# Half tiles of 64 tokens in an attention kernel: two heads in one unit of 128 partitions

## The chip, the cores and the metric

The kernel runs on one core of one Trainium2 chip. The metric is the device time of one execution in microseconds, the median of several runs. Five engines work side by side on a core: TensorE (PE, with PEld for its weight loads), VectorE (DVE), ScalarE (ACT), GpSimd (POOL) and SyncE (SP), which issues all DMAs here.

## The reference

Attention with rotary positions over 4 batches, 8 heads, 576 positions and a head width of 64, then a two-layer network with a leaky ramp on the 2304 tokens of 512 values:

```python
q_rot, k_rot = rotate(q), rotate(k)
scores = q_rot @ k_rot.T / sqrt(D)              # (4, 8, 576, 576)
attn = exp(scores - max(scores)); attn = attn / (sum(attn) + 1e-09)
x = (attn @ v).transpose(0, 2, 1, 3).reshape(B * S, H * D)
h = x @ w_in                                    # (2304, 512) @ (512, 2048)
g = maximum(h, 0.0) + alpha * minimum(h, 0.0)
return g @ w_out                                # (2304, 2048) @ (2048, 512)
```

## The kernel before

The 2304 tokens are cut into 18 tiles of 128. A batch has 576 tokens, four tiles and a half, so tiles 4 and 13 lie across two batches and are cut into two parts of 64 tokens, with partitions 0 to 63 for the first batch and 64 to 127 for the second. All other tiles are one part. Two tiles form a block of 256 tokens, nine in all.

Attention works on pairs of heads. `pair` (L642) takes one part of a tile and two heads that share a tile of keys (`ks`, one head on rows 0 to 63, the other on rows 64 to 127). It issues four score products (L653, two halves of 288 keys for each head, on 64 rows of the array, fp32), each head into its own two banks of PSUM. The products always take all 128 tokens of the tile, the other batch's too, and `head` (L661) then uses the partitions `a:z` of the part. For each head `head` makes one unit: maximum over the 576 scores (L665, VectorE), exponential with its sum (L674, ScalarE), the fp16 high part (L679, ScalarE or VectorE), the low part (L693, VectorE), a transpose by DMA (L697, SyncE) and 14 products with the values (L703). With 64 tokens a unit is as long as with 128; it only uses half the partitions. Each of tiles 4 and 13 has 2 parts x 8 heads = 16 such units, a whole tile has 8, so there are 160 units in all. `normalise` (L710) scales a part's sums by 1/sum (`rs`, shown at the line of the helper `scalar`, L352) and splits the result into fp16 high and low (`xs`, L722 and L724), which are transposed into `xt`.

`expert` (L736) does the network for one block in 16 slices of 128 hidden values: twelve products of layer 1 (L745, in two halves of six), the ramp on ScalarE (L756) and VectorE (`r`, L759), and layer 2. For blocks 0 and 1 layer 2 is two fp32 products of 512 columns (L765, two instructions each); from block 2 on it is six products (L783) of `r` split into `gh` and `gl`. Attention of block i + 1 runs between the slices of block i. The first quarter of the span also loads the weights and converts them from 64-bit words, mostly on VectorE (L506 to L515, L580, L584).

Nothing is ordered by hand. `Plan` (L68) collects all operations with a due time, the engines that may do them and a modelled cost, and runs a model of the five engines that picks the next operation for each; the program is issued in that order. The table `PRM` (L35) holds due times and costs. VectorE and GpSimd are modelled as taking turns on one port, except for operations marked `port=False`; `small` (L347) marks its VectorE operations so, among them `rs`. Each buffer is reused in the order of the plan, and an operation waits for the users of the buffer before.

## Time and profile before

| | us |
|---|---|
| median of 3 runs | 695.69 |
| lowest, highest | 694.82, 698.32 |
| the profiled execution, its own time | 700.17 |
| its span, first to last instruction | 698.4 |

| engine | busy, us | share of the span |
|---|---|---|
| TensorE | 620.2 | 89% |
| VectorE | 522.8 | 75% |
| ScalarE | 354.7 | 51% |
| GpSimd | 194.8 | 28% |

Busy time is the time in which an engine executes. A product is given an end by a model, so a busy TensorE may still be short of its peak. "Idle before" is the time in which the engine had nothing to do just before a group, and the releaser is what ended the wait. The granted clock (PEclk) is a share of TensorE's full 2.4 GHz.

### The profile page before, as it was taken

How to read it: one execution, taken by the hardware profiler on the slowest of the kernel's cores; microseconds unless marked ns; L12 is line 12 of the kernel's file. 1: busy time of each engine (PE TensorE's matmuls, PEld its weight loads, DVE VectorE, ACT ScalarE, POOL GpSimd, SP SyncE). 2: the span in 40 equal slices, each digit the busy share in tenths (PEclk: the TensorE clock that was granted, in tenths of full speed). 3: DMA queues.
4: the chain of work that ended last, by engine and by line, in shares of the span. 5: the costliest groups of instructions: out<-in, count | busy, mean ns of one | idle time of the engine just before them, and what ended most of it. 6: DMA issues, size and time to landing. Idle time of an engine off the chain costs nothing.

```text
span 698.4 us, 14088 instructions
## 1 busy us (share of the span) xinstructions
PE 620.2 (89%) x5448; PEld 445.0 (64%) x5448; DVE 522.8 (75%) x898; ACT 354.7 (51%) x799; POOL 194.8 (28%) x149
## 2 busy tenths in 40 slices
PE   0756678769998999999999999999999999999997
PEld 0434444346555666776767777776777777777775
DVE  5988999999889876768896485777976757765332
ACT  3536756549763535444664544444665444643322
POOL 3753100204735331235623121352232212010000
PEclk9965569979999999999999999999999999999999
DMA  8999798685885676547896465683466545453000
GB/s 291 309 228 215 156 290 217 184 263 130 143 185 97 119 129 137 94 99 176 199 206 106 99 112 98 119 180 47 78 108 115 100 77 93 100 110 58 31 1 31
DMA packets 209523, 96.48 MB, mean 138 GB/s; under 512 B 192304, under 2 KB 196528, under 8 KB 209456
## 3 DMA queue, kind: packets, MB, share of 16 engines
q1 hardware_dynamic: 209456, 95.59, 63.0%
q8 instruction: 42, 0.69, 0.4%
q14 instruction: 25, 0.20, 0.1%
HBM read 41.56 MB, written 4.72 MB: 66 GB/s over the span
## 4 chain that ended last, share of the span: by engine, by line
PE 62%; DMA 17%; DVE 16%; issue 2%; SPq 1%; ACT 1%; POOL 0%; ACTq 0%; DVEq 0%; POOLq 0%
PE h L745 22%; PE pair L783 20%; DMA pt<-pp 11%; PE pair L653 8%; PE v L703 7%; PE pair L765 5%; DVE pp L693 3%; DVE mx L665 2%; DMA wraw<-in_moe_w_in_dram 2%; DMA qr<-in_q_dram 1%; DMA kraw<-in_k_dram 1%; DVE wi L584 1%; DVE wo L515 1%; DVE r L759 1%; DVE pp L352 1%
## 5 line engine op out<-in xcount | busy, mean ns | idle before, releaser
L745 PE MATMUL h<-xt,wi 128*128 128x256 f16 x1728 | 231.1, 277 | 14.8 <-DVE r L759 14.4
L745 PEld LDWEIGHTS <-wi 128*128 128x128 f16 x1728 | 155.8, 99 | 76.2 <-issue 59.0
L674 ACT ACTIVATE e<-pair,mx 128x576 f32<-128x576 f32 (+1 forms) x160 | 117.2, 736 | 89.2 <-DVE mx L665 85.7
L693 DVE SCALAR_TENSOR_TENSOR pp<-e,pp 128x576 f16<-128x576 f32 (+1 forms) x160 | 136.0, 858 | 13.6 <-ACT pp L679 11.9
L759 DVE SCALAR_TENSOR_TENSOR r<-r,beta,h 128x256 f32<-128x256 f32 x144 | 68.6, 476 | 78.7 <-ACT r L756 78.0
L665 DVE TENSOR_REDUCE mx<-pair 128x1 f32<-128x576 f32 (+1 forms) x160 | 114.1, 750 | 13.3 <-PE pair L653 12.6
L703 PE MATMUL v<-vv,pt 128*128 128x64 f16 (+1 forms) x2240 | 93.5, 198 | 30.1 <-DMA pt<-pp 29.7
L756 ACT ACTIVATE r<-h 128x256 f32<-128x256 f32 x144 | 55.1, 382 | 127.5 <-PE h L745 125.0
L703 PEld LDWEIGHTS <-pt 128*128 128x128 f16 (+1 forms) x2240 | 83.8, 104 | 56.4 <-DMA pt<-pp 43.7
L653 PE MATMUL pair<-ks,qn 64*128 64x288 f32 x640 | 112.4, 458 | 5.8 <-ACT e L674 4.8
L783 PE MATMUL pair<-wh,gh 128*128 128x512 f32 x224 | 96.4, 430 | 0.1
L783 PE MATMUL pair<-wh,gl 128*128 128x512 f32 x224 | 88.8, 397 | 1.6 <-POOL gl L776 1.6
L776 POOL TENSOR_TENSOR gl<-r,gh 128x256 fp32r<-128x256 f32 x55 | 53.3, 969 | 129.4 <-ACT gh L773 108.4
L783 PE MATMUL pair<-wo,gh 128*128 128x512 f32 x224 | 88.1, 393 | 0.0
L653 PEld LDWEIGHTS pair<-ks,qn 64*128 64x128 f32 x640 | 61.4, 198 | 40.8 <-issue 15.1
L679 ACT ACTIVATE pp<-e 128x576 f16<-128x576 f32 (+1 forms) x97 | 65.5, 681 | 19.6 <-DMA pt<-pp 15.6
L773 ACT ACTIVATE gh<-r 128x256 fp32r<-128x256 f32 x100 | 41.7, 417 | 56.7 <-PE pair L783 28.6
L765 PE MATMUL pair<-wo,r 128*128 128x512 f32 x128 | 63.4, 622 | 0.0
L783 PEld LDWEIGHTS pair<-wh,gl 128*128 128x128 f32 x224 | 42.3, 189 | 12.2 <-POOL gl L776 2.4
L724 POOL TENSOR_TENSOR xs<-y,xs 128x512 f16<-128x512 f32 (+1 forms) x18 | 25.2, 1398 | 86.5 <-DVE xs L722 65.1
L783 PEld LDWEIGHTS pair<-wh,gh 128*128 128x128 f32 x224 | 42.5, 190 | 10.4 <-issue 2.7
L636 POOL TENSOR_TENSOR qn<-qr 128x512 f32<-128x512 f32 (+1 forms) x19 | 24.0, 1265 | 87.7 <-PE pair L653 87.7
(70 smaller groups left out, 533.8 us busy)
## 6 DMA issues: line engine op xcount, KB each, us to landing
kraw<-in_k_dram SPq DMA_DIRECT2D x16, 576.0 KB, 4.8
qr<-in_q_dram SPq DMA_DIRECT2D x18, 512.0 KB, 4.3
wraw<-in_moe_w_in_dram SPq DMA_DIRECT2D x16, 512.0 KB, 5.7
wraw<-in_moe_w_out_dram SPq DMA_DIRECT2D x16, 512.0 KB, 6.5
vraw<-in_v_dram SPq DMA_DIRECT2D x16, 320.0 KB, 4.3
out_dram<-os SPq DMA_DIRECT2D x18, 256.0 KB, 2.6
pt<-pp SPq DMA_TRANSPOSE x160, 3.4
vv<-vv SPq DMA_DIRECT2D x32, 64.0 KB, 2.2
```

Of the source, the lines that this page charges most:

```text
L653: nc.tensor.matmul(out=ps[h]()[:, x, :HS], lhsT=qn()[r, p], rhs=kt()[r, x * HS:(x + 1) * HS], start=True, stop=True)
L665: lambda e: nc.vector.tensor_reduce(out=mx()[a:z], in_=ps()[a:z, :, :HS], axis=AX.XY, op=ALU.max, negate=True),
L674: lambda e: nc.scalar.activation(out=ex()[a:z].rearrange("p (x c) -> p x c", x=2), in_=ps()[a:z, :, :HS], func=ACTF.Exp, bias=mx()[a:z], a ...
L679: lambda e: nc.scalar.activation(out=pp()[a:z, 0], in_=ex()[a:z], func=ACTF.Copy, scale=1.0 if early else E_SC) if e == ACT
L693: lambda e: nc.vector.scalar_tensor_tensor(out=pp()[a:z, 1], in0=ex()[a:z], scalar=E_SC, in1=pp()[a:z, 0], op0=ALU.mult, op1=ALU.subtract),
L703: nc.tensor.matmul(out=v_b()[a:z, i], lhsT=pt()[:, s, :z - a], rhs=vt()[:, h, w], start=(n == 0), stop=(n == len(order) - 1))
L745: nc.tensor.matmul(out=ps(), lhsT=wi_b()[:, kk, j // FG, w, f], rhs=x()[:, y * KC + kk], start=(kk == 0 and n == 0), stop=(kk == KC - 1 an ...
L756: lambda e: nc.scalar.activation(out=g(), in_=ps(), func=ACTF.Relu, scale=-1.0),
L759: lambda e: nc.vector.scalar_tensor_tensor(out=g(), in0=g(), scalar=beta_b()[:, j:j + 1], in1=ps(), op0=ALU.mult, op1=ALU.add),
L765: nc.tensor.matmul(out=po()[:, x], lhsT=g()[:, x * 128:(x + 1) * 128], rhs=wf[j](), start=(j == 0), stop=(j == KF - 1))
L776: lambda e: ENG[e].tensor_tensor(out=gl(), in0=g(), in1=gh().bitcast(F32), op=ALU.subtract),
L783: nc.tensor.matmul(out=po()[:, x], lhsT=s()[:, ts], rhs=w, start=(j == 0 and c == 0), stop=(j == KF - 1 and c == 2))
```

## The change

A part of 64 tokens goes to the new `half_pair`. It keeps a square of 128 x 128 for each pair of heads (`qd`, one buffer for a part's four pairs): the 64 queries of the first head stand in rows and columns 0 to 63, those of the second in rows and columns 64 to 127, and the rest is zero. ScalarE copies the queries in (two copies a part), GpSimd or VectorE fills in the zeros (two fills a part). Two score products on all 128 rows then give both heads, the first on partitions 0 to 63, the second on 64 to 127, in one PSUM bank pair. `head` is called once for both heads, so a part has 4 units instead of 8; 144 are left in all. The sums of a part go into a tile `st` with a column for each pair, and two VectorE copies a part bring them to the partitions where `normalise` reads them (`sums`). The weighted sums are still two runs of 14 products, one for each head, from the two halves of the unit's transposed tile.

The table's new numbers are `wl2` 12.07, `wb2` 4.87, `kd` 2.73, `wg` 3.2, `ph0` 3.06, `lw` 3.8, `la` 2, `ka` 2.03, `vp` 1.47 and `gl` 10.88.

```diff
--- before.py
+++ after.py
-PRM = {"qd": 7.03, "qd0": 3.48, "vl0": 32.45, "wl": 12.02, "wl2": 24.13, "wb": 10.45, "wb2": 4.75, "ws": -0.7, "ws2": -0.08, "kl": 40.87, "vl": 40.84, "lead": 3.61, "flow": 4, "pen": -3.74, "ph": 1.2, "xlo": 1.8, "kd": 3.03, "pl": 1.01, "wlo": 16.77, "wg": 2.88, "bk": 1500, "lead1": 2.25, "ph0": 4.16, "nb": 1, "wh": 8.51, "lw": 3.65, "pvd": 4.03, "pw": 3.28, "la": 4, "lv": 1, "nks": 5, "nvv": 5, "ka": 6.08, "va": 0.1, "vc": -2.76, "vp": 1.57, "qa": 0.5, "qr": 78.54, "tqk": 1340, "l2d": 3.34, "tl2": 1400, "nos": 2, "nr": 2, "fo": 4, "fi": 4, "gh": 21.96, "gl": 11.78, "gh0": -1.64, "gl0": 1.86, "tp": 0, "nf": 2, "sh": 8.29, "sl": 2.28, "tl": 0, "wpe": 0, "vpe": 1, "wk": 4.09}
+PRM = {"qd": 7.03, "qd0": 3.48, "vl0": 32.45, "wl": 12.02, "wl2": 12.07, "wb": 10.45, "wb2": 4.87, "ws": -0.7, "ws2": -0.08, "kl": 40.87, "vl": 40.84, "lead": 3.61, "flow": 4, "pen": -3.74, "ph": 1.2, "xlo": 1.8, "kd": 2.73, "pl": 1.01, "wlo": 16.77, "wg": 3.2, "bk": 1500, "lead1": 2.25, "ph0": 3.06, "nb": 1, "wh": 8.51, "lw": 3.8, "pvd": 4.03, "pw": 3.28, "la": 2, "lv": 1, "nks": 5, "nvv": 5, "ka": 2.03, "va": 0.1, "vc": -2.76, "vp": 1.47, "qa": 0.5, "qr": 78.54, "tqk": 1340, "l2d": 3.34, "tl2": 1400, "nos": 2, "nr": 2, "fo": 4, "fi": 4, "gh": 21.96, "gl": 10.88, "gh0": -1.64, "gl0": 1.86, "tp": 0, "nf": 2, "sh": 8.29, "sl": 2.28, "tl": 0, "wpe": 0, "vpe": 1, "wk": 4.09}
...
+    qd_T = tag("qd", 1, [128, NP, 128], F32)
+    st_T = tag("st", 2, [128, NP], F32)
...
     def pair(at, step, t, b, p, a, z, banks):
-        if t not in sums:
-            sums[t], ys[t], xss[t], vos[t] = sums_T.new(), y_T.new(), xs_T.new(), v_T.new()
         kt, vt, qn = ks[b, p], vv[b, p], qs[t]
+        if z - a < 128:
+            return half_pair(at, t, b, p, a, z, banks[p % 2])
         ps = [x.new() for x in banks]
...
-    def head(at, t, p, h, a, z, ps, vt):
-        sm, v_b, i = sums[t], vos[t], 2 * p + h
+    qds, sts = {}, {}
+
+    def half_pair(at, t, b, p, a, z, bank):
+        kt, vt, qn = ks[b, p], vv[b, p], qs[t]
+        if (t, a) not in qds:
+            qd, sts[t, a] = qd_T.new(), st_T.new()
+            qds[t, a] = qd
+            for h in range(2):
+                o, c = 64 * h, 64 - 64 * h
+                op(at - 2, {POOL: 420, DVE: (t_dve(256, fast=True), 1)},
+                   lambda e, o=o, c=c: ENG[e].memset(qd()[o:o + 64, :, c:c + 64], 0.0), writes=[(qd, h)])
+                op(at - 2, {ACT: t_act(256)},
+                   lambda e, o=o: nc.scalar.activation(out=qd()[o:o + 64, :, o:o + 64], in_=qn()[o:o + 64, :, a:z], func=ACTF.Copy),
+                   reads=[(qn, 0), (qn, 2)], writes=[(qd, 2 + h)])
+        qd, ps = qds[t, a], bank.new()
+
+        def scores(e):
+            for x in range(2):
+                nc.tensor.matmul(out=ps()[:, x, :HS], lhsT=qd()[:, p], rhs=kt()[:, x * HS:(x + 1) * HS], start=True, stop=True)
+
+        op(at, {PE: 980}, scores, kind=WIDE, reads=[(qd, x) for x in range(4)] + [kt], writes=[ps])
+        head(at, t, p, None, a, z, ps, vt)
+        if p == NP - 1:
+            st, sm = sts[t, a], sums[t]
+            for h in range(2):
+                small(at + 0.8, lambda h=h: nc.vector.tensor_copy(
+                    out=sm()[a:z].rearrange("p (c x) -> p c x", x=2)[:, :, h], in_=st()[64 * h:64 * h + 64]),
+                    reads=[(st, x) for x in range(NP)], writes=[(sm, (2 * x + h, a)) for x in range(NP)])
+            normalise(at + 0.8, t, b, a, z)
+
+    def head(at, t, p, h, c, d, ps, vt):
+        both = h is None
+        a, z = (0, 128) if both else (c, d)
+        if t not in sums:
+            sums[t], ys[t], xss[t], vos[t] = sums_T.new(), y_T.new(), xs_T.new(), v_T.new()
+        v_b = vos[t]
+        if both:
+            acc, acc_of = lambda: sts[t, c]()[:, p:p + 1], (sts[t, c], p)
+        else:
+            acc, acc_of = lambda: sums[t]()[a:z, 2 * p + h:2 * p + h + 1], (sums[t], (2 * p + h, a))
...
-               bias=mx()[a:z], accum_out=sm()[a:z, i:i + 1]),
-           reads=[ps, mx], writes=[ex, (sm, (i, a))])
+               bias=mx()[a:z], accum_out=acc()),
+           reads=[ps, mx], writes=[ex, acc_of])
...
-        def pv(e):
-            order = [(s, s) for s in [0, *range(NH, NSEG), *range(1, NH)]] + [(s, NSEG + s) for s in range(NH)]
+        order = [(s, s) for s in [0, *range(NH, NSEG), *range(1, NH)]] + [(s, NSEG + s) for s in range(NH)]
+
+        def pv(e, g, o):
             for n, (s, w) in enumerate(order):
                 nc.tensor.matmul(
-                    out=v_b()[a:z, i], lhsT=pt()[:, s, :z - a], rhs=vt()[:, h, w],
+                    out=v_b()[c:d, 2 * p + g], lhsT=pt()[:, s, o:o + d - c], rhs=vt()[:, g, w],
                     start=(n == 0), stop=(n == len(order) - 1))
 
-        op(at + (0.6 if t < 4 else PRM["pvd"]), {PE: 430}, pv, kind=SHORT,
-           reads=[pt] + [(vt, x) for x in range(4)], writes=[(v_b, (i, a))])
+        for g, o in [(0, 0), (1, 64)] if both else [(h, 0)]:
+            op(at + (0.6 if t < 4 else PRM["pvd"]), {PE: 430}, lambda e, g=g, o=o: pv(e, g, o), kind=SHORT,
+               reads=[pt] + [(vt, x) for x in range(4)], writes=[(v_b, (2 * p + g, c))])
```

The order that the plan makes of it, at three places. First VectorE in the middle of block 0's experts, where the last slices of `w_in` and `w_out` are converted (`wraw`, `wi`, `wo`); `r` is the ramp's result, which layer 2 and the next layer 1 wait for. Before:

```order
L515 SCALAR_TENSOR_TENSOR wraw<-wraw,wi 128x512
L511 SCALAR_TENSOR_TENSOR wo<-wraw,wo 128x512
L693 SCALAR_TENSOR_TENSOR pp<-e,pp 128x576
L515 SCALAR_TENSOR_TENSOR wo<-wraw,wo 128x512
L540 TENSOR_REDUCE cm<-wm 128x1
L506 TENSOR_SCALAR wo<-wraw 128x512
L364 STREAM_TRANSPOSE ct<-cm 128x32
L759 SCALAR_TENSOR_TENSOR r<-r,beta,h 128x256
```

After:

```order
L735 SCALAR_TENSOR_TENSOR pp<-e,pp 128x576
L517 SCALAR_TENSOR_TENSOR wraw<-wraw,wi 128x512
L508 TENSOR_SCALAR wo<-wraw 128x512
L803 SCALAR_TENSOR_TENSOR r<-r,beta,h 128x256
L513 SCALAR_TENSOR_TENSOR wo<-wraw,wo 128x512
L542 TENSOR_REDUCE cm<-wm 128x1
L508 TENSOR_SCALAR wo<-wraw 128x512
```

The `r` has moved ahead of two steps of the conversion of `wo` and of the first steps that find the weights' bound.

Second VectorE where the first part of tile 4 ends. `sums` are the sums of exponentials, `rs` their reciprocal, `ve` the bound of the next batch's values. Before:

```order
L364 STREAM_TRANSPOSE ct<-cm 128x32
L365 TENSOR_REDUCE cr<-ct 128x1
L357 MEMSET cm 128x32
L693 SCALAR_TENSOR_TENSOR pp<-e,pp 64x576
L759 SCALAR_TENSOR_TENSOR r<-r,beta,h 128x256
L352 TENSOR_SCALAR ve<-pair_2038 128x1
L352 TENSOR_SCALAR rs<-sums 64x8
L352 TENSOR_SCALAR ve<-ve 128x1
L715 RECIPROCAL rs<-rs 64x8
```

After:

```order
L393 TENSOR_TENSOR ks<-kraw 128x576
L366 STREAM_TRANSPOSE ct<-cm 128x32
L393 TENSOR_TENSOR ks<-kraw 128x576
L690 COPY sums<-st 64x4 x2
L367 TENSOR_REDUCE cr<-ct 128x1
L735 SCALAR_TENSOR_TENSOR pp<-e,pp 128x576
L354 TENSOR_SCALAR rs<-sums 64x8
```

The two copies of the sums stand ahead of `rs`, between two additions of the rotated keys (`ks`) and the search for the values' bound.

Third the beginning of tile 13. `kraw` are the keys times the rotation table, `xs` the high part of the tile before, `gl` the low part of `r`. VectorE before:

```order
L717 TENSOR_TENSOR y<-v,rs 128x512
L722 CAST xs<-y 128x512
L759 SCALAR_TENSOR_TENSOR r<-r,beta,h 128x256
L724 TENSOR_TENSOR xs<-y,xs 128x512
L665 TENSOR_REDUCE mx<-pair_5923 64x1
L391 TENSOR_TENSOR ks<-kraw 128x576
L665 TENSOR_REDUCE mx<-pair_5925 64x1
```

VectorE after:

```order
L707 TENSOR_REDUCE mx<-pair_5777 128x1
L390 TENSOR_TENSOR kraw<-kraw,tab 128x1152
L354 TENSOR_SCALAR pp<-e 128x576
L761 TENSOR_TENSOR y<-v,rs 128x512
L803 SCALAR_TENSOR_TENSOR r<-r,beta,h 128x256
L735 SCALAR_TENSOR_TENSOR pp<-e,pp 128x576 x2
L803 SCALAR_TENSOR_TENSOR r<-r,beta,h 128x256
```

GpSimd at the same place, before:

```order
L391 TENSOR_TENSOR ks<-kraw 128x576
L776 TENSOR_TENSOR gl<-r,gh 128x256
L388 TENSOR_TENSOR kraw<-kraw,tab 128x1152
L776 TENSOR_TENSOR gl<-r,gh 128x256
L391 TENSOR_TENSOR ks<-kraw 128x576
```

and after:

```order
L393 TENSOR_TENSOR ks<-kraw 128x576
L820 TENSOR_TENSOR gl<-r,gh 128x256 x2
L393 TENSOR_TENSOR ks<-kraw 128x576
L768 TENSOR_TENSOR xs<-y,xs 128x512
L820 TENSOR_TENSOR gl<-r,gh 128x256
L675 MEMSET qd 64x4x64 x2
L820 TENSOR_TENSOR gl<-r,gh 128x256 x2
```

The multiplication `kraw` has moved from GpSimd to VectorE, ahead of `y`; VectorE's CAST of `xs` is gone from it (ScalarE does it now), and GpSimd does the low part of `xs` and the zero fills.

## Rows read from the trace of the kernel before

**Rows 1.** The page, part 1: engine, busy us, share of span, instructions.

```profile
PE 620.2 (89%) x5448; PEld 445.0 (64%) x5448; DVE 522.8 (75%) x898; ACT 354.7 (51%) x799; POOL 194.8 (28%) x149
```

**Rows 2.** Stretches: length; busy us (instructions) by engine; PEclk, DMA share, GB/s.

```profile
149.90:264.20 114.30, 106.25 (x930) 66.38 (x928) 99.25 (x164) 66.56 (x143) 46.77 (x28) 0.99 0.71 137
...
264.20:466.60 202.40, 196.24 (x1863) 149.55 (x1861) 146.43 (x253) 103.53 (x245) 65.37 (x55) 1.00 0.66 134
...
466.60:575.70 109.10, 106.41 (x1020) 79.86 (x1019) 82.61 (x141) 56.08 (x132) 29.83 (x26) 0.98 0.52 91
...
475.00:480.00 5.00, 5.00 (x30) 3.59 (x27) 3.69 (x7) 2.81 (x7) 0.00 (x0) 0.72 0.56 55
```

**Rows 3.** The chain that ended last: start us, us, engine, tile, line, instructions.

```profile
213.33 1.72 PE pair L765 x4
...
215.05 1.17 PE pair L653 x8
...
456.67 1.42 PE h L745 x12
...
482.82 1.40 PE pair L783 x6
...
490.20 1.00 PE v L703 x28
...
516.08 0.56 PE v L703 x14
```

**Rows 4.** Groups by line and shape: count, busy us, mean ns, idle before, releaser.

```profile
L665 DVE TENSOR_REDUCE mx<-pair 64x1 f32<-64x576 f32 x32 | 23.0, 749 | 3.9 <-PE pair L653 3.6
...
L693 DVE SCALAR_TENSOR_TENSOR pp<-e,pp 64x576 f16<-64x576 f32 x32 | 27.1, 858 | 4.8 <-ACT pp L679 4.4
...
L756 ACT ACTIVATE r<-h 128x256 f32<-128x256 f32 x144 | 55.1, 382 | 127.5 <-PE h L745 125.0 <-PE pair L765 1.5 <-POOL gl L776 0.2
...
L388 DVE TENSOR_TENSOR kraw<-kraw,tab 128x1152 f32<-128x1152 f32 x4 | 5.8, 1442 | 2.5 <-DMA kraw<-in_k_dram 2.5
...
L722 DVE CAST xs<-y 128x512 f16<-128x512 f32 x11 | 6.9, 630 | 0.1
...
L357 POOL MEMSET cm<- 128x32 f32 x6 | 0.9, 156 | 59.0 <-DVE ct L364 58.7 <-POOLq L924 0.3
...
L773 ACT ACTIVATE gh<-r 128x256 fp32r<-128x256 f32 x100 | 41.7, 417 | 56.7 <-PE pair L783 28.6 <-DVE r L759 26.8
...
L352 DVE TENSOR_SCALAR rs<-sums 128x8 f32<-128x8 f32 x16 | 4.2, 264 | 0.9 <-ACT e L674 0.9
```

**Rows 5.** Timeline of TensorE, 149.9 to 264.2 us: start us, us, work, [idle before, releaser].

```profile
152.20 0.82 PE L745 MATMUL h<-xt,wi 128*128 128x256 f16 x6 [2.26 <-DVE r L759]
...
164.02 0.81 PE L745 MATMUL h<-xt,wi 128*128 128x256 f16 x6 [0.91 <-DVE r L759]
...
207.09 0.63 PE L703 MATMUL v<-vv,pt 128*64 128x64 f16 x14 [1.23 <-DMA pt<-pp]
...
225.36 1.47 PE L745 MATMUL h<-xt,wi 128*128 128x256 f16 x12 [1.75 <-DVE r L759]
```

**Rows 6.** Timeline of VectorE and GpSimd in the same stretch.

```profile
151.71 0.43 DVE L759 SCALAR_TENSOR_TENSOR r<-r,beta,h 128x256 f32<-128x256 f32 x1
...
222.42 2.31 DVE L352 TENSOR_SCALAR rs<-sums 64x8 f32<-64x8 f32 x1
...
222.03 2.67 POOL L630 TENSOR_TENSOR qr<-qr,tab 128x1024 f32<-128x1024 f32 x1
```

**Rows 7.** Timeline of VectorE, GpSimd and TensorE from 469 to 474 us.

```profile
469.79 2.71 DVE L722 CAST xs<-y 128x512 f16<-128x512 f32 x1
...
469.60 2.62 POOL L388 TENSOR_TENSOR kraw<-kraw,tab 128x1152 f32<-128x1152 f32 x1 [1.25 <-DMA kraw<-in_k_dram]
...
472.94 0.81 PE L745 MATMUL h<-xt,wi 128*128 128x256 f16 x6 [2.08 <-DVE r L759]
```

## The prediction

> **What bounds the kernel now.** I read the page's engine table first: TensorE is busy 89% of the span, VectorE 75% [rows 1], so TensorE is the engine to follow and its idle time is what can be won besides its work. Next I asked where the change acts at all. Set side by side, the order of every engine before and after is word for word the same up to the middle of block 0's experts, again over the whole middle, and again at the end; TensorE's order differs in two stretches only. A runs from 149.9 to 264.2 us of the profiled execution and holds tile 4, B from 466.6 to 575.7 us and holds tile 13: the two tiles that lie across two batches and are cut into parts of 64 tokens. (The new numbers of the table, early loads included, move nothing before A.) So I cut the span there and read busy time by stretch [rows 2]: in A TensorE is busy 106.25 of 114.30 us, idle 8.05; in B 106.41 of 109.10, idle 2.69. VectorE is busy 99.25 us in A (87%) and 82.61 us in B (76%). Both stretches are bound by TensorE, with gaps that VectorE causes. What the change can win is TensorE work taken out of A and B, and a part of these gaps; what it can lose is new gaps there.
>
> **The change part by part.**
>
> *Score products.* A pair of half tiles (16 pairs, 8 in A and 8 in B) gives up four products on 64 rows of the array for two on 128. The chain shows one pair as 1.17 us for eight instructions [rows 3]. The new shape, fp32 on 128 rows, is that of the first experts' second layer: 1.72 us for four instructions of 512 columns [rows 3], 0.43 each; at 288 columns 0.43 x 288/512 = 0.242, four of them 0.97 us. Saving 0.20 x 16 = **-3.2 us**, all on the path since TensorE is the bound. Ends: 0 if the new form costs as much as the old, -3.2 if it scales by columns; I take -3.2, because that row has the same rows, type and weight load.
>
> The Trainium skill ("TensorEngine Tiling (Array Packing)", Overview) speaks against this edit: with a contraction of 64 or less the array is to be packed by rows, for up to twice the rate. By that the packed pair would cost what two full products cost, 0.97 us, and zero padding would win nothing; the trace shows 1.17, so I go by the row and keep the rule as a rival below.
>
> *Softmax units.* 32 units of 64 partitions become 16 of 128. On VectorE each unit's maximum takes 749 ns and its low part 858 ns [rows 4], whatever the partitions, so 16 x 1.61 = 25.7 us of VectorE work go, 12.9 in each stretch. ScalarE and the transposes lose units likewise. None of this is on the path by itself: it counts only as gaps that close.
>
> *TensorE's pieces.* The weighted sums keep their number (two heads of 14 products for each new unit), but as two heads become ready together, in B 24 runs of them become 17. A run of 14 takes 0.56 us, a run of 28 1.00 [rows 3]: 0.12 for each merging, 7 x 0.12 = **-0.8 us**. In A the count stays at 24.
>
> *VectorE's order at the start of A.* TensorE waits 2.26 us before 152.20 and 0.91 us before 164.02 for VectorE's r [rows 5]. Both r's now stand further ahead: the first before two steps of the conversion of w_out (order above), the second before the L584 conversions of w_in. The first cannot come before ScalarE's 382 ns [rows 4] and its own 0.43 us [rows 6], so about 1.0 us of the 2.26 stays: -1.2; the second gap should close: -0.9. Together **-2.1 us**.
>
> *The stall in B.* VectorE's CAST at 469.79 takes 2.71 us and ends when GpSimd's multiplication of the keys, begun at 469.60 for 2.62 us, ends [rows 7]; the other ten CASTs of that line take 0.42 us on the mean ((11 x 0.630 - 2.71)/10 [rows 4]). The r queued behind it comes late, TensorE waits 2.08 us [rows 7], and from 475 to 480 us the granted clock is 0.72 [rows 2], partly 1.2 GHz instead of 2.4: 5 x 0.28 = 1.4 us more. In the new order VectorE does that multiplication itself (1442 ns [rows 4], into the 26 us in which it is idle in B) and the CAST has left it. **-3.5 us**; ends 0 (another such meeting in its place) and -3.5.
>
> *The other gaps of A.* 8.05 - 2.26 - 0.91 = 4.9 us are left, the largest 1.23 us on a transpose and 1.75 us on an r [rows 5]; the second is again a stall, rs at 222.42 held 2.31 us by GpSimd's qr of 222.03 [rows 6]. With 12.9 us less on VectorE I take half: **-2.4 us**, ends 0 and -4.9.
>
> *What is added.* Eight zero fills of 64 x 256 values and eight ScalarE copies into the square. The nearest rows are GpSimd's fill of 128 x 32 at 156 ns and ScalarE's copy of 256 columns at 417 ns [rows 4]. Only the second part of a tile can wait for them: there is one square, and it is free after the first part's fourth score product. Queued behind ScalarE's copies are an r or some weight splits. In A TensorE has 56 products of weighted sums and two second-layer steps between the two (2 x 1.00 + 2 x 1.72 = 5.4 us [rows 3]), in B six second-layer products, 56 of weighted sums and 12 of the first layer (1.40 + 2 x 1.00 + 1.42 = 4.8 us). Two fills and two copies are below 2 x 1 + 2 x 0.42 = 2.9 us even with a fill at 1 us, so I cost them at nothing; with that cover gone, two waits of about 3 us. Then VectorE copies eight sums of 64 x 4. The nearest row is rs of 128 x 8, 264 ns on the mean with stalls in it [rows 4]: 8 x 0.26 = 2.1 us of VectorE. The planner books them as not meeting GpSimd, as it did rs. Those of A stand among GpSimd's qn, kraw and qr (order above), so I expect one of four places to stall TensorE like the 1.75 and 2.08 us above: **+2.0 us**, and **+1.0 us** for waits of a new order that I don't foresee. Ends 0 and +5.
>
> What pages say of it: the Trainium skill ("SBUF — State Buffer", the part on engine and AXI ports) calls the port pair of VectorE and GpSimd an exclusive lock held for a whole instruction, the loser fully blocked. The two stalls read above agree; the slower rival below is that mechanism, priced from rows.
>
> **Sum.** -3.2 - 0.8 - 2.1 - 3.5 - 2.4 + 3.0 = -9.0 us. The profiled execution's own time, 700.17 us for a span of 698.4, becomes 691.2. It lies 4.5 us above the median of the runs, 695.69; I take the same difference from the median: 686.7 us. Some of the stalls may be shorter in the median run, which is one more reason for a wide upper end.
>
> **Rivals.**
>
> 1. *The scores win nothing* (the packed pair is as good as two full products, by the page named above). The rest stays: -5.8, 689.9 us. For it: packing is what two heads of 64 rows invite. Against: 1.17 against 0.97 us, both at full clock. 12%.
>
> 2. *The gaps come back elsewhere.* TensorE's work shrinks, but a newly planned order has waits as long as the old one, and only scores, pieces and about nothing else are won, less 3 us of added work and stalls: -1.0, 694.7 us. For it: between A and B, where VectorE is busy only 146.43 of 202.40 us, TensorE still idles 6.2 us [rows 2], so a lighter VectorE is no warrant for a full TensorE. 22%.
>
> 3. *All gaps of A close and nothing new comes:* -3.2 - 0.8 - 2.1 - 3.5 - 4.9 = -14.5, 681.2 us. 12%.
>
> 4. *Slower: the copies of the sums meet GpSimd.* All four places stall by a GpSimd instruction's length, each costing TensorE 2.08 us as in B [rows 7], 8.3 in all, and the terms that rest on VectorE's order (-2.1, -3.5, -2.4) are lost with it, since every r queued behind a copy is late: -4.0 + 8.3 = +4.3, 700.0 us. It decides from the third stalled place on. For it: rs, booked the same way, stalled 2.31 us. Against: in B GpSimd has only short steps near the copies, and most of the sixteen rs of 128 x 8 run clean (264 ns mean). 8%.
>
> 5. *It doesn't do what it says:* the two parts can't run as units of two heads. The order shows 16 fewer maxima and 16 pairs of products on qd, so I give it no chance of its own.
>
> **How the numbers follow.** The forecast, 686.7 us, has 46%. Its own bounds: scores 0 instead of -3.2, other gaps 0 instead of -2.4, additions +5 instead of +3 give 694.3; additions 0 and the other gaps -4.9 give 681.2. The range reaches to rivals 2 and 3 and leaves out rival 4 and some tails: 680.5 to 694.7 us. A difference of 0.5% (3.5 us) is about what a measurement of this kernel tells from none: faster is below 692.2 (forecast, 1, 3: 70%), the same is 692.2 to 699.2 (rival 2: 22%), slower above 699.2 (8%).
>
> **What would show it.** In the changed kernel's profile the score products on qd should take 0.97 us for four instructions in the chain; 1.17 means rival 1. Stretch A should be some 5 us shorter, B some 4 to 5. The stall before 472.94 and the low clock behind it should be gone. The copies of sums should take about 0.2 us each; several over 1 us, with TensorE waiting for r behind them, mean rival 4. TensorE's idle time in A should be near 4 us; 8 means rival 2. The middle, 202.4 us between A and B, and the 122.7 us after B should not change. If they do, the argument from the order is wrong.

## The result, and the profile after

The changed kernel takes 686.46 us, the median of 4 runs (684.13 to 688.93), where the kernel before took 695.26 beside it (694.44 to 698.32): a ratio of 0.9866, 95% interval 0.9818 to 0.9914, 8.8 us less. Medians are of all executions of a kernel; the ratios leave out the few that ran in a slower state. The forecast was 686.7. The time is right; three of the steps that lead to it are not, and they are the reason to read on.

The engine table of the changed kernel (engine, busy us, share of the span, instructions), against [rows 1]:

```profile
PE 608.4 (89%) x5384; PEld 443.8 (65%) x5384; DVE 507.9 (74%) x879; ACT 339.9 (50%) x766; POOL 181.0 (27%) x145
```

TensorE has 11.8 us less to do and is as full as before. Its chain shows the new score products, against the 1.17 us of [rows 3] (start, us, engine, tile, line, instructions):

```profile
450.57 0.97 PE pair L683 x4
455.05 1.94 PE pair L683 x8
```

The groups by line and shape show what was added, and the copy of xs that had stalled, against [rows 4]:

```profile
L683 PE MATMUL pair<-ks,qd 128*128 128x288 f32 x64 | 17.8, 409 | 0.0
...
L766 DVE CAST xs<-y 128x512 f16<-128x512 f32 x9 | 3.8, 423 | 0.1
L677 ACT ACTIVATE qd<-qn 64x256 f32<-64x256 f32 x8 | 3.3, 414 | 1.2 <-PE pair L683 1.1
...
L690 DVE COPY sums<-st 64x4 f32<-64x4 f32 x8 | 2.4, 302 | 0.8 <-ACT e L716 0.7
L675 POOL MEMSET qd<- 64x256 f32 x7 | 2.1, 305 | 1.5 <-PE pair L683 1.3
```

No copy of xs is stalled any more (423 ns on the mean, 630 before). TensorE's timeline in A and in B, the waits of about a microsecond and more, against [rows 5] and [rows 7]:

```profile
141.55 1.47 PE L789 MATMUL h<-xt,wi 128*128 128x256 f16 x12 [1.02 <-DVE r L803]
147.79 2.72 PE L789 MATMUL h<-xt,wi 128*128 128x256 f16 x12 [2.64 <-DVE r L803]
162.26 0.58 PE L746 MATMUL v<-vv,pt 128*128 128x64 f16 x14 [1.13 <-DMA pt<-pp]
175.47 0.58 PE L746 MATMUL v<-vv,pt 128*128 128x64 f16 x14 [1.74 <-DMA pt<-pp]
191.10 1.47 PE L789 MATMUL h<-xt,wi 128*128 128x256 f16 x12 [1.26 <-DVE r L803]
234.30 0.58 PE L746 MATMUL v<-vv,pt 128*128 128x64 f16 x14 [1.35 <-DMA pt<-pp]
...
471.04 1.07 PE L746 MATMUL v<-vv,pt 128*64 128x64 f16 x28 [1.29 <-DMA pt<-pp]
482.62 1.07 PE L746 MATMUL v<-vv,pt 128*64 128x64 f16 x28 [0.40 <-DMA pt<-pp]
509.88 0.58 PE L746 MATMUL v<-vv,pt 128*128 128x64 f16 x14 [0.98 <-DMA pt<-pp]
```

The 2.08 us before tile 13's layer 1 are gone. A has as many waits as before, and B has three new ones, of weighted sums (v) for transposed probabilities (pt). One of A's is a new stall. VectorE's and GpSimd's timelines, and what they hold up:

```profile
186.44 2.64 POOL L390 TENSOR_TENSOR kraw<-kraw,tab 128x1152 f32<-128x1152 f32 x1 [5.16 <-DVE xu L354]
186.54 3.75 DVE L390 TENSOR_TENSOR kraw<-kraw,tab 128x1152 f32<-128x1152 f32 x1
190.58 0.47 DVE L803 SCALAR_TENSOR_TENSOR r<-r,beta,h 128x256 f32<-128x256 f32 x1
```

**A mistake in the prediction comes first.** It let B begin at 466.6 us of before. TensorE's order is the same only up to about 459.3 us, some 7 us earlier. So from here on stretches are cut by work and not by time: layer 1 has 144 slices of twelve products in the whole program, and A runs from the first product of slice 9 to that of slice 33, B from slice 82 to slice 110. The two rows of before at these marks (length; busy us and instructions by engine; PEclk, DMA share, GB/s):

```profile
144.60:269.20 124.60, 114.98 (x1001) 71.54 (x1001) 108.34 (x179) 71.89 (x155) 46.77 (x28) 0.99 0.71 142
461.90:581.80 119.90, 116.81 (x1141) 88.44 (x1140) 89.99 (x154) 60.93 (x145) 35.43 (x30) 0.99 0.52 94
```

and those of the changed kernel:

```profile
141.50:262.00 120.50, 112.11 (x969) 72.12 (x969) 99.90 (x169) 62.60 (x135) 40.55 (x29) 0.99 0.68 146
451.40:567.00 115.60, 112.68 (x1117) 88.72 (x1116) 83.25 (x147) 55.30 (x129) 30.64 (x25) 1.00 0.53 100
```

A is 4.1 us shorter, B 4.3. TensorE idles 8.4 us in A, against 9.6; 2.9 in B, against 3.1. A holds the same work in both but for the scores; B does not quite. In the changed kernel six products of layer 2 that stood ahead of slice 82 stand behind it. The second layer's instructions alone, in B of before and of the changed kernel:

```profile
461.90:581.80 119.90, 45.58 (x168) 30.64 (x168) 0.99 0.52 94
451.40:567.00 115.60, 45.91 (x174) 31.20 (x174) 1.00 0.53 100
```

Six of these take 1.4 us (0.23 from the start of one to the next, in the timeline), so B really won 5.7 us, and the stretch between A and B lost 1.4 us of work.

### The profile page after: what moved, and what is told of

It is laid out like the page before. It is cut to its first block, busy times and chain, and to the rows that moved or that the text cites. A ratio compares the mean times of both kernels' runs of the same rounds, so it can differ in the third digit from the quotient of the medians.

```text
span 682.3 us, 13828 instructions
## 1 busy us (share of the span) xinstructions
PE 608.4 (89%) x5384; PEld 443.8 (65%) x5384; DVE 507.9 (74%) x879; ACT 339.9 (50%) x766; POOL 181.0 (27%) x145
## 4 chain that ended last, share of the span: by engine, by line
PE 68%; DMA 18%; DVE 10%; issue 1%; ACT 1%; SPq 1%; POOL 0%; ACTq 0%; DVEq 0%; POOLq 0%
PE h L789 24%; PE pair L827 21%; DMA pt<-pp 14%; PE v L746 8%; PE pair L655 8%; PE pair L809 5%; PE pair L683 2%; DVE kraw L390 1%; DMA qr<-in_q_dram 1%; DMA kraw<-in_k_dram 1%; DVE pp L735 1%; DVE mx L707 1%; DVE wi L586 1%; DMA wraw<-in_moe_w_out_dram 1%; DVE wraw L517 1%
## 5 line engine op out<-in xcount | busy, mean ns | idle before, releaser
L716 ACT ACTIVATE e<-pair,mx 128x576 f32<-128x576 f32 x144 | 105.6, 736 | 87.7 <-DVE mx L707 83.5
L735 DVE SCALAR_TENSOR_TENSOR pp<-e,pp 128x576 f16<-128x576 f32 x144 | 126.1, 882 | 8.1 <-ACT pp L721 7.0
L707 DVE TENSOR_REDUCE mx<-pair 128x1 f32<-128x576 f32 x144 | 103.2, 750 | 11.7 <-PE pair L655 10.3
L655 PE MATMUL pair<-ks,qn 64*128 64x288 f32 x512 | 89.4, 453 | 7.2 <-ACT e L716 6.2
L820 POOL TENSOR_TENSOR gl<-r,gh 128x256 fp32r<-128x256 f32 x49 | 48.3, 986 | 116.5 <-ACT gh L817 80.1
L655 PEld LDWEIGHTS pair<-ks,qn 64*128 64x128 f32 x512 | 48.8, 196 | 35.5 <-issue 12.5
L721 ACT ACTIVATE pp<-e 128x576 f16<-128x576 f32 x90 | 61.1, 681 | 15.8 <-DMA pt<-pp 14.8
L809 PE MATMUL pair<-wo,r 128*128 128x512 f32 x128 | 61.7, 607 | 0.0
L768 POOL TENSOR_TENSOR xs<-y,xs 128x512 f16<-128x512 f32 (+1 forms) x19 | 27.8, 1463 | 109.9 <-DVE xs L766 85.9
L820 DVE TENSOR_TENSOR gl<-r,gh 128x256 fp32r<-128x256 f32 x63 | 28.7, 456 | 26.2 <-ACT gh L817 25.5
```

The source lines that it names most:

```text
L655: nc.tensor.matmul(out=ps[h]()[:, x, :HS], lhsT=qn()[r, p], rhs=kt()[r, x * HS:(x + 1) * HS], start=True, stop=True)
L707: lambda e: nc.vector.tensor_reduce(out=mx()[a:z], in_=ps()[a:z, :, :HS], axis=AX.XY, op=ALU.max, negate=True),
L716: lambda e: nc.scalar.activation(out=ex()[a:z].rearrange("p (x c) -> p x c", x=2), in_=ps()[a:z, :, :HS], func=ACTF.Exp, bias=mx()[a:z], a ...
L721: lambda e: nc.scalar.activation(out=pp()[a:z, 0], in_=ex()[a:z], func=ACTF.Copy, scale=1.0 if early else E_SC) if e == ACT
L735: lambda e: nc.vector.scalar_tensor_tensor(out=pp()[a:z, 1], in0=ex()[a:z], scalar=E_SC, in1=pp()[a:z, 0], op0=ALU.mult, op1=ALU.subtract),
L809: nc.tensor.matmul(out=po()[:, x], lhsT=g()[:, x * 128:(x + 1) * 128], rhs=wf[j](), start=(j == 0), stop=(j == KF - 1))
```

## The experiments

All runs were compared with the kernel before on the same chip. The table has the ratio of each to it, and from its trace the same two rows as above, as length = TensorE busy + idle. The median of before was between 695.3 and 699.5 us.

| run | median us | ratio, 95% interval | A | B |
|---|---|---|---|---|
| before (profile shown above) | 695.26 | | 124.6 = 115.0 + 9.6 | 119.9 = 116.8 + 3.1 |
| again_before | 699.23 | 1.0009 (0.9970 to 1.0048) | 122.1 = 115.4 + 6.7 | 119.8 = 116.8 + 3.0 |
| after (profile shown above) | 686.46 | 0.9866 (0.9818 to 0.9914) | 120.5 = 112.1 + 8.4 | 115.6 = 112.7 + 2.9 |
| again_after | 687.55 | 0.9868 (0.9828 to 0.9908) | 120.2 = 112.3 + 7.9 | 115.5 = 112.8 + 2.7 |
| new_form_old_numbers | 687.37 | 0.9865 (0.9826 to 0.9904) | 118.6 = 112.6 + 6.0 | 115.1 = 112.8 + 2.3 |
| old_form_new_numbers | 702.45 | 1.0066 (1.0036 to 1.0096) | 128.6 = 116.5 + 12.1 | 116.0 = 115.0 + 1.0 |
| merged_only_in_A | 689.38 | 0.9881 (0.9841 to 0.9921) | 118.5 = 112.1 + 6.4 | 116.1 = 114.7 + 1.4 |
| merged_only_in_B | 689.96 | 0.9885 (0.9843 to 0.9926) | 122.5 = 115.8 + 6.7 | 114.2 = 112.6 + 1.6 |
| stall_of_B_moved | 694.09 | 0.9945 (0.9913 to 0.9977) | 125.6 = 116.9 + 8.7 | 115.7 = 114.9 + 0.8 |
| packed_scores | 689.59 | 0.9883 (0.9854 to 0.9912) | 123.1 = 115.5 + 7.6 | 115.8 = 114.5 + 1.3 |
| packed_old_numbers | 690.06 | 0.9864 (0.9845 to 0.9882) | 120.7 = 112.2 + 8.5 | 115.7 = 114.5 + 1.2 |
| copies_doubled | 686.59 | 0.9862 (0.9824 to 0.9899) | 121.5 = 112.6 + 8.9 | 115.3 = 112.7 + 2.6 |
| r_first_in_A | 690.48 | 0.9901 (0.9862 to 0.9940) | 124.2 = 115.3 + 8.9 | 115.4 = 112.7 + 2.7 |
| pieces_later_in_B | 684.34 | 0.9799 (0.9777 to 0.9821) | 120.2 = 112.6 + 7.6 | 113.2 = 113.0 + 0.2 |

How to read it: B repeats within 0.1 to 0.2 us from one execution of a program to the next (119.9 and 119.8; 115.6 and 115.5). Over the five programs that have the changed kernel's order in B (after and again_after count as one; copies_doubled differs by its doubled steps alone) it is 115.1 to 115.6 and once 114.2, in merged_only_in_B. A repeats only within some 2.5 us (124.6 and 122.1), and so does the rest of the program: the stretch between slices 46 and 60, far from the change, took 60.3 to 63.2 us. Two microseconds in B are therefore a finding; a microsecond in A or in a median is not. The runs were made on several chips, so times of different runs are compared by their ratios.

### The form of the units or the new numbers

The first run is the kernel before unchanged, the second the changed one.

> The kernel before once more, for a second trace of it. All theories expect the median of before, about 695.3 us, a ratio of 1.00. In the first traces the stretch before A, where nothing changed, already differed by 3 us and the middle by 1.7 us. If these differences are chance, this trace shows them too: slice starts of layer 1 that move by 2 to 4 us between two executions of the same program. The stall of the CAST in front of tile 13 (2.71 us, TensorE waiting 2.08 us) should come again at its place if the order makes it, and be gone or shorter if it was chance.

> The changed kernel once more: about 686.5 us, ratio 0.987. The stretch of tile 13 should again be shorter than in before by some 5 to 6 us and tile 4's by some 4 us; if the first trace was a lucky one, it is the stretches without a change that grow back, not these two.

The third is the changed kernel with the old table of numbers, the fourth the kernel before with the new one. The edit of the fourth, the entries that differ (the third has it the other way round):

```diff
-"ka": 6.08, "kd": 3.03, "la": 4, "wl2": 24.13, "gl": 11.78, "ph0": 4.16, "wg": 2.88, "wb2": 4.75, "lw": 3.65, "vp": 1.57
+"ka": 2.03, "kd": 2.73, "la": 2, "wl2": 12.07, "gl": 10.88, "ph0": 3.06, "wg": 3.2, "wb2": 4.87, "lw": 3.8, "vp": 1.47
```

> The half-tile units with the table's numbers of before. Its order differs from the changed kernel's in stretch A alone. If the form of the units wins the time (scores -3.2 us, the rest by fewer units), this keeps most of it: 686 to 690 us. If the newly tuned numbers win it, it falls back towards before: 691 to 695 us.

> The units of before with the table's new numbers, the other half of the change. If the form wins the time, this is within 2 us of before (693 to 698 us). If the numbers win it, it is near the changed kernel: 687 to 690 us.

The form with the old numbers has the whole gain, 0.9865; the numbers alone cost 0.7%; in the one trace A is the longest of all (128.6 us, 12.1 of them idle). So what follows may be tried with the old numbers. One thing in the fourth run is a hint: its B is 116.0, as short as with the new form, though the units there are the old ones.

### One stretch at a time

```diff
-        if z - a < 128:
+        if z - a < 128 and t == 4:
```

and the same with `t == 13`, both with the old numbers.

> Two heads share a unit only in the half tile at token 560 (stretch A); the half tile at token 1632 (stretch B) keeps the old form, and the numbers are the old ones, so that from the middle of the program on TensorE's order is that of before. The prediction's steps put into A one half of the scores and of the TensorE pieces (1.6 and 0.4 us), the normalised read that moved ahead (2.1) and half of the other gaps (2.4), less half of what is added (1.5): 5.0 us less than before, 0.993 of it, and the stretch between the slices 9 and 33 of layer 1 some 5 us shorter. A rival theory, by which the whole gain comes from the stall of B that is gone and A's gaps are only moved about: within 2 us of before, 0.997 to 1.003.

> Two heads share a unit only in the half tile at token 1632 (stretch B), with the old numbers; up to the middle of the program TensorE's order is that of before. The prediction's steps give B one half of the scores and pieces (2.0 us) and the stall behind the copy of xs with its stretch of lower clock (3.5), less half of what is added (1.5): 4.0 us less than before, 0.994 of it, and slices 82 to 110 some 4 us shorter. The theory that the two stretches add up gives 9 us for this run's gain and that of the run with the form in A alone together. A rival, by which a stretch that is shorter gives its gain back in the next one: the two gains sum to well over or under the 9 us that both forms together give.

The two gains of merged_only_in_A and merged_only_in_B, 1.19% and 1.15%, together would be 16 us, and both forms at once give 9. That looks like the rival, by which a gain is given back in the next stretch, and is not. With the form in A alone, A gets 118.5 and **B gets 116.1 as well**, 3.7 less than before, and there the orders of TensorE, VectorE, ScalarE and GpSimd are those of before, instruction by instruction. What differs is a time, and the 2.71-us copy of xs isn't there. The place at tile 13 in this run (timelines of VectorE and GpSimd):

```profile
463.74 0.43 DVE L766 CAST xs<-y 128x512 f16<-128x512 f32 x1
464.08 0.48 DVE L803 SCALAR_TENSOR_TENSOR r<-r,beta,h 128x256 f32<-128x256 f32 x1
...
465.75 2.53 DVE L393 TENSOR_TENSOR ks<-kraw 128x576 f32<-128x576 f32 x1
...
464.62 3.05 POOL L390 TENSOR_TENSOR kraw<-kraw,tab 128x1152 f32<-128x1152 f32 x1 [2.35 <-DMA kraw<-in_k_dram]
```

In the two traces of before, GpSimd's pass over the keys (kraw) began 0.2 and 0.1 us ahead of the copy. Here it begins 0.9 us behind the copy's start and finds it over: the transfer of the keys took 4.3 us from issue to landing, not 3.7. VectorE is held by the pass all the same, but later, in an addition of keys (2.53 us for ks, 1.28 in before), behind r and with no wait of TensorE after it. The fourth run of the section above shows why its B was as short. There the pass begins 0.1 us behind the copy, as its transfer took 4.2 us:

```profile
472.16 0.43 DVE L722 CAST xs<-y 128x512 f16<-128x512 f32 x1
472.29 2.78 POOL L388 TENSOR_TENSOR kraw<-kraw,tab 128x1152 f32<-128x1152 f32 x1 [1.59 <-DMA kraw<-in_k_dram]
472.50 0.48 DVE L759 SCALAR_TENSOR_TENSOR r<-r,beta,h 128x256 f32<-128x256 f32 x1
472.90 2.71 DVE L724 TENSOR_TENSOR xs<-y,xs 128x512 f16<-128x512 f32 x1
```

The copy, begun first, runs clean; so does r, in the middle of the pass; the low part of xs takes the 2.71 us, and TensorE doesn't wait for it. So GpSimd's pass still stalls VectorE in these two runs, but behind r. Why the transfer took half a microsecond longer is open, and there is one trace of each. The gain of B's stall is thus in both runs with the form in one stretch, which is why they don't add up. (The form in B alone leaves A as it was, 122.5, and takes B to 114.2; the rest of that run's median lies within its interval.)

### What B's stall is worth

The stall is no accident of one execution. In again_before it stands at the same place, in the timelines of GpSimd, VectorE and TensorE:

```profile
464.04 2.62 POOL L388 TENSOR_TENSOR kraw<-kraw,tab 128x1152 f32<-128x1152 f32 x1 [1.34 <-PE h L745]
464.15 2.79 DVE L722 CAST xs<-y 128x512 f16<-128x512 f32 x1
...
467.38 0.81 PE L745 MATMUL h<-xt,wi 128*128 128x256 f16 x6 [2.17 <-DVE r L759]
```

```diff
-        op(at, {DVE: t_dve(DM, fast=True), ACT: t_act(DM)},
+        op(at, {ACT: t_act(DM)} if t == 12 else {DVE: t_dve(DM, fast=True), ACT: t_act(DM)},
```

> The kernel before with one edit: the copy of xs (128 by 512, to 16 bits) that VectorE makes behind the read of tile 12 is made by ScalarE. All of TensorE's order but a few instructions behind that place is that of before. The copy took 2.71 us on VectorE beside GpSimd's pass over 128 by 1152, and TensorE waited 2.08 us behind it and then ran 5 us at a lower clock. If the stall costs what the prediction put on it: 2.1 to 3.5 us less than before, a ratio of 0.995 to 0.997, and TensorE's wait at that place and the lower clock behind it are gone. The rival, that VectorE is held by GpSimd's pass whatever it runs there, so that the next instruction on VectorE takes the wait over: a VectorE instruction of over 2 us stands there in the copy's place, and the time is that of before within 0.2%.

0.9945, 3.8 us of 698.05, and B is 4.2 us shorter. In the copy's place VectorE now makes the pass over the keys itself, and ScalarE the copy:

```profile
469.67 1.35 DVE L388 TENSOR_TENSOR kraw<-kraw,tab 128x1152 f32<-128x1152 f32 x1
469.72 0.39 ACT L756 ACTIVATE r<-h 128x256 f32<-128x256 f32 x1 [1.88 <-PE h L745]
470.00 0.62 ACT L721 ACTIVATE xs<-y 128x512 f16<-128x512 f32 x1
```

The edit so moves two things at once, as the planner gave the pass to VectorE of itself; with either the two instructions can no longer meet. It doesn't test the rival, that VectorE is held whatever it runs, since GpSimd makes no pass there; the traces above do: the pass holds a copy, an addition or a low part that begins behind it, and not r. TensorE's idle time in B falls by 2.2 us and its busy time by 1.9: the second is the lower clock behind the wait (0.99 over the stretch, 1.00 without).

### The form of the scores

```diff
-                nc.tensor.matmul(out=ps()[:, x, :HS], lhsT=qd()[:, p], rhs=kt()[:, x * HS:(x + 1) * HS], start=True, stop=True)
+                for h in range(2):
+                    r = slice(64 * h, 64 * h + 64)
+                    nc.tensor.matmul(out=ps()[r, x, :HS], lhsT=qn()[r, p, a:z], rhs=kt()[r, x * HS:(x + 1) * HS], start=True, stop=True)
```

The square, its fills and its copies of q are left out with it.

> The changed kernel with its new numbers and its merged units, but the scores of a pair of heads are four products of 64 rows and 64 columns of TensorE, as before, and not two of 128: the zeroed square and the copies of q onto its diagonal are gone. If the score term of the prediction is right (0.20 us for each of 16 products in a pair), this takes some 3.2 us more than the changed kernel, less the 0.1 to 2 us of copies that it saves: 1.2 to 3.1 us more, a ratio to before of 0.989 to 0.992 against 0.987. The group of four products takes 1.17 us again and not 0.97. The rival, that the smaller products run side by side and win as much by themselves: the group takes 0.97 or less, and the time is the changed kernel's or below it.

> The run with packed scores once more (four products of 64 rows and 64 columns for a pair, no zeroed square and no copies of q), on the chip and beside the run above: its group of eight products took 1.12 to 1.17 us there, against 0.97 for four on the square, while its time was 1.2 us over the changed kernel with intervals of 2.5 us on either side. If the score term is worth what the groups say (0.15 to 0.20 us for 16 pairs): 2.4 to 3.2 us over the changed kernel, a ratio of 0.990. If packing is as good in time, whatever the groups take: 0.987.

The second run is the same kernel on another chip, with the new numbers too; its label is a slip. In the chain two pairs, sixteen products, take 2.09 us, where two on the square take 1.94 in B and 2.02 in A:

```profile
165.55 2.09 PE pair L676 x16
461.86 2.09 PE pair L676 x16
```

That is 1.05 us for a pair. Where a pair stands alone, the timelines of packed_scores, of before and of the changed kernel have

```profile
472.77 1.19 PE L676 MATMUL pair<-ks,qn 64*64 64x288 f32 x8
460.75 1.24 PE L653 MATMUL pair<-ks,qn 64*128 64x288 f32 x8
480.44 1.13 PE L683 MATMUL pair<-ks,qd 128*128 128x288 f32 x4
```

So narrower products were a little cheaper than expected, and the square is cheaper still. In B, where all other products of the two kernels are the same in number, TensorE is busy 1.8 us longer with the packed form (114.5 against 112.7), 0.26 for each of the seven pairs in it. But it idles 1.5 us less, so only 0.2 us arrive. In the whole time the square's gain is not shown: the ratios, 0.9883 and 0.9864 against 0.9866 and 0.9868, differ by less than their intervals, and the second run gave the 0.987 that stood for packing being as good, not 0.990. The ten times of the packed kernel have a median of 689.8, the ten of the changed one 687.5, but on other chips. The square saves work; whether it saves time, these runs don't settle.

### What the added steps cost

Every fill and every copy twice, as in

```diff
-                   lambda e, o=o, c=c: ENG[e].memset(qd()[o:o + 64, :, c:c + 64], 0.0), writes=[(qd, h)])
+                   lambda e, o=o, c=c: [ENG[e].memset(qd()[o:o + 64, :, c:c + 64], 0.0) for _ in range(2)], writes=[(qd, h)])
```

> The changed kernel with each zero fill, each copy of q onto the square's diagonal and each copy of the sums made twice in a row, by the same engine at the same place: 8 fills, 8 ScalarE copies and 8 VectorE copies more, every engine's order otherwise that of the changed kernel. If the added steps are hidden, as the trace of the changed kernel suggests (no TensorE wait behind a copy): within 0.5 us of the changed kernel, a ratio to before of 0.987. If they cost what the prediction put on them (2.0 us for stalls of the sums' copies), the doubling costs another 2.0 us: a ratio of 0.990. The slower rival (every copy of sums stalls TensorE 2.08 us at its four places): 8.3 us more, 0.999.

0.9862, 686.59 us: the added steps cost nothing that can be measured, though the interval is some 2.6 us wide to either side and so could hide the 2.0 us. B, which repeats better, is 115.3 us long, as without the doubling. VectorE's copies of the sums do get stalled now and then (352 ns on the mean, 1.26 us the longest), and the trace shows nothing that waits for them:

```profile
L677 ACT ACTIVATE qd<-qn 64x256 f32<-64x256 f32 x16 | 6.6, 414 | 1.4 <-PE pair L683 1.1
L690 DVE COPY sums<-st 64x4 f32<-64x4 f32 x16 | 5.6, 352 | 3.0 <-ACT e L716 2.7
```

### A's waits for r

In new_form_old_numbers one r of A waits 3.83 us on VectorE, from 147.58 to 151.41, behind steps of the weights' conversion. The rows of ScalarE, VectorE and TensorE:

```profile
147.19 0.39 ACT L800 ACTIVATE r<-h 128x256 f32<-128x256 f32 x1 [0.38 <-PE h L789]
...
151.41 0.44 DVE L803 SCALAR_TENSOR_TENSOR r<-r,beta,h 128x256 f32<-128x256 f32 x1
...
151.90 0.81 PE L789 MATMUL h<-xt,wi 128*128 128x256 f16 x6 [1.72 <-DVE r L803]
```

So the r's were put ahead in that kernel:

```diff
-        op(at + 0.2, {DVE: t_dve(256, 1)},
+        op(at + (0.2 if i else -4), {DVE: t_dve(256, 1)},
```

> The changed form of the units with the old numbers, and the planner's due time of VectorE's r for the first 256 tokens 4.2 steps earlier, so that an r whose input is there goes ahead of the conversion steps of the experts' weights. In the run with the new form and the old numbers, TensorE waited 1.48, 1.72 and 1.39 us for three r's in stretch A, whose inputs from ScalarE were there 0.94, 3.83 and 0.73 us before VectorE began them. If these waits are what the order of VectorE costs: 0.94 + 1.72 + 0.73 = 3.4 us less than that run, a ratio to before of 0.982 against 0.987, and TensorE idle some 4 us in A instead of 6. The rival, that VectorE's backlog moves the wait to what now stands behind the r's (the maxima and low parts of the softmax, so the transposes): A's idle time stays 6 to 8 us and the time within 1 us of that run.

The theory fails: 0.9901 against 0.9865 for the run it starts from, 2.5 us slower by the ratios, whose intervals overlap. The rival holds in that the waits come back: A is 124.2 us long, against 118.6. Of the waits for r at 144, 152 and 163 us the first shrinks to 1.14, the second to 0.32, the third goes, and others stand in their place. TensorE's timeline, and its clock behind the longest of them (windows of 5 us):

```profile
162.41 1.24 PE L683 MATMUL pair<-ks,qd 128*128 128x288 f32 x4 [1.89 <-ACT e L716]
...
172.22 0.93 PE L746 MATMUL v<-vv,pt 128*128 128x64 f16 x14 [3.70 <-DMA pt<-pp]
```

```profile
165.00:170.00 5.00, 3.39 (x28) 2.21 (x28) 5.00 (x5) 5.00 (x12) 4.78 (x4) 1.00 1.06 220
170.00:175.00 5.00, 2.79 (x35) 2.42 (x36) 4.79 (x5) 2.88 (x7) 4.92 (x4) 0.61 0.87 209
175.00:180.00 5.00, 5.00 (x20) 2.87 (x18) 1.08 (x3) 3.51 (x8) 1.04 (x1) 0.70 0.76 188
```

The 3.70 us are a wait for transposed probabilities. VectorE, busy for the whole window ahead, had ended their low part by 166.03 us, and the transposition was issued at 166.11. From issue to landing it took

```profile
DMA to landing us min/median/max: 6.1/6.1/6.1
```

where the median of the kernel is 3.4; the share of the DMA engines is 1.06 there. With a usual transposition the wait would have been about 1.0 us (an estimate: 3.70 less the 2.7 it ran over). So the rival's reason, VectorE's backlog, holds for little of this wait. The changed kernel's wait of 1.74 us at 175.47 is of the same kind: its transposition took 6.6 us.

### B's new waits

```diff
-            op(at + (0.6 if t < 4 else PRM["pvd"]), {PE: 430}, lambda e, g=g, o=o: pv(e, g, o), kind=SHORT,
+            op(at + (0.6 if t < 4 else PRM["pvd"] + (1.5 if both and t == 13 else 0)), {PE: 430}, lambda e, g=g, o=o: pv(e, g, o), kind=SHORT,
```

> The changed kernel with one due time moved: in the half tile at token 1632 the weighted sums of a merged unit are due 1.5 steps later, so that TensorE has other work ahead of them while the transposed probabilities of the two heads are on their way. In the changed kernel TensorE's idle time in stretch B is 2.9 us, of which 2.7 are three waits of the sums for a transposition; the kernel before without its stall idles 0.8 there. Theory: these waits are a price of the merged unit that a later due time avoids: slices 82 to 110 take some 113.5 us instead of 115.6, and the time is 2 us lower, a ratio to before of 0.984. Rival: the sums then come late for the unit's normalising, TensorE waits there or the work only moves: 115.6 us again and a ratio of 0.987.

B takes 113.2 us, less than in any other run, TensorE is idle 0.2 of them, and the kernel is faster than both: 684.34 us, a ratio of 0.9799 (0.9777 to 0.9821), below the changed kernel's median of 687.5 by 3.1 us and by 4.7 if the ratios are compared:

```profile
454.00:567.20 113.20, 113.01 (x1118) 88.69 (x1117) 80.31 (x143) 57.43 (x133) 28.48 (x25) 1.00 0.55 102
```

2.4 us of this are B's. The rest is of the size of the chance in a median, since the program before and behind B hardly differs. What the waits are, the changed kernel's chain shows:

```profile
466.09 4.90 DMA pt<-pp
```

The transpositions that TensorE waits for in B took 4.9, 3.8 and 4.8 us from issue to landing; the median is 3.4. The waits of 1.29, 0.40 and 0.98 are of the size of what they ran over.

## Why the prediction was right, step by step

**Where the gain lies** was half right. The forecast's terms put -4.6 us in A and -4.4 in B, if half of the +3.0 goes to each. B won 5.7 (4.3, and the 1.4 us of layer 2 that it took over). A was 123.7 us on the mean of the four traces with the old form and the old numbers in it, 120.6 in the four with the changed kernel's order: 3.1, not the 4.1 of the first pair. The middle and the tail were to stay. From slice 33 to 82 it was 192.7 and 190.6 us in the two traces of before, 189.4 and 191.1 in two of after, which the six products explain. Behind slice 110 it was 111.7 and 111.9 against 110.9 and 111.1, with the orders of TensorE, VectorE, ScalarE and GpSimd the same in before and after. About half of that is a wait for one transposition (0.47 us at 637.12 in before), absent after; why is open.

**Score products, -3.2.** The row was as predicted, 0.97 us, and the first rival, that the old pair is as good, has fallen in work: the old pair took 1.17 in the chain, and packing by columns too 1.05. What the square is worth in time over packed products is not shown.

**Merged pieces, -0.8.** TensorE's busy time in B is 114.9 us in stall_of_B_moved, where no low clock disturbs, and 112.7 after, with 1.4 us of layer 2 added: scores and pieces together took 3.6 us out. Seven pairs at 0.20 (the eighth stands ahead of slice 82) and 0.8 for the pieces, all of which the prediction put in B, are 2.2, so the two terms together were too small.

**The stall in B, -3.5,** was the best step: 3.8 us by the times and 4.2 by the stretch, in the run that parts the two instructions. But it is no property of the new form. With other numbers, or with an edit in A, the old form loses it as well: a shift of under a microsecond put it behind r.

**The r's moved ahead, -2.1, and the other gaps, -2.4,** are the steps that failed. The old form idled 6.7 to 9.6 us in A (four traces with the old numbers), the changed order 7.6 to 8.9 (four traces): nothing, where 4.5 had been booked. The r that was to wait 1.0 us waits 2.64 in the first trace of after and 0.90 in the second; new are waits for transpositions, the longest for one of 6.6 us, and the stall of VectorE's pass, 3.75 us, at 186.54. (In the second trace the roles change there: VectorE's pass, begun first, takes 1.34 us, a high part behind it 2.89 instead of 0.46, and TensorE waits 1.30 us for the same r.) Here the second rival was right. The error was to count a wait as won because the instruction stands further ahead in the order, and to take half of the rest for a lighter VectorE; r_first_in_A shows what such a shift does. VectorE had less relief, too, than the 12.9 us booked: its busy time in A fell from 108.3 to 99.9 us, by 8.4. And not all gaps hang on VectorE: the longest new wait is for a transfer.

**What is added, +3.0.** The copies' cost does not show (copies_doubled), so the +2.0 was in the wrong place. The +1.0 for waits that weren't foreseen was too small: in B they are 2.1 us (idle 2.9 against 0.8 without the stall). That a later due time takes them away is shown (pieces_later_in_B). That they come of merging is not: the probabilities of two heads are transposed as one, and such a transposition takes longer (2.7 to 2.9 us for six of tile 13's in before, 3.2 at least in the changed kernel), but the packed kernel has the same merged units and idles only 1.2 to 1.3 us in B, and merged_only_in_B, with the changed kernel's order there, 1.6.

So B is: -4.2 for the stall, -3.6 for scores and pieces, +1.4 for the products that it took over, +2.1 for the new waits, -4.3 in all. The forecast had -3.5, -2.4 and, by half, +1.5, the last for another reason. In A the gaps were to give 4.5 and gave none; instead TensorE's busy time fell by 3.4 us (115.0 to 116.9 in the old form, 112.1 to 112.6 in the new) where the scores' 1.6 had been booked. About 1.1 of this is no work saved: the 96 products of layer 2 in A, the same in all kernels, take 46.1 to 46.9 us in the four traces of the old form and 45.4 and 45.3 in two of the new. The granted clock is 0.97 to 0.99 in the former and 0.99 in the latter; what the rest is, these runs don't settle. With the new numbers A is 120.2 to 121.5 long in four traces, with the old numbers and the new form 118.5 and 118.6: the numbers seem to cost A some 2 us, which the medians don't confirm (687.55 and 687.37). That the sum came within 0.3 us of the measurement is luck: 4.5 us that A's gaps didn't give stood against work that fell further than booked, and added costs that were partly of another kind.

**The level** was carried from the profiled execution to the median by a fixed 4.5 us. The changed kernel's profiled executions took 684.13 and 689.52 for medians of 686.46 and 687.55, 2.3 us below the one and 2.0 above the other, so the offset is chance and no quantity to carry.

## What to carry to other kernels

When an edit shifts two engines against each other, ask first which stalls of the old order it breaks: one meeting of VectorE and GpSimd ahead of a critical instruction was worth 4.2 us here, more than the work saved in the same stretch (3.6). And ask whether it is broken or only moved: in two traces here a stall behind the instruction that TensorE waits for held up nothing, and half a microsecond in a transfer decided it. Where an engine beside the critical one is nearly full, book saved work on the critical engine and no closed gaps; in this kernel the gaps moved. And where TensorE waits for a transfer's result, try a later due time for the consumer before anything else: 1.5 steps took B's idle time from 2.9 to 0.2 us.

## What the runs showed of the hardware

The meeting of VectorE and GpSimd came in both executions of before: 2.71 and 2.79 us for the same copy, 0.42 elsewhere. The r, which reads h, the products' result, ran in 0.48 us in the middle of the pass that held the low part of xs behind it for 2.71 (old_form_new_numbers). It also works between equals: VectorE's pass over 128 by 1152 took 3.75 us beside GpSimd's of 2.64, and 1.36 alone:

```profile
459.00 1.36 DVE L390 TENSOR_TENSOR kraw<-kraw,tab 128x1152 f32<-128x1152 f32 x1 [1.11 <-DMA kraw<-in_k_dram]
```

A wait of TensorE costs more than itself. Behind 3.70 us of idling in r_first_in_A the clock was 0.61 and 0.70 in two windows of 5 us, a mix of 1.2 and 2.4 GHz, and TensorE's busy time in A rose by 2.7 us with as many instructions; behind the 2.1 us in B it cost 1.9 more. And products of 64 columns of weights went a little faster than those of 128 on the same 64 rows, 1.19 us against 1.24 in the timeline for a group of eight. Transpositions of probabilities took 2.7 us at least with 64 partitions and 3.2 at least with 128, from issue to landing, and up to 7.8 us in the changed kernel.
